# A six-layer cross network on one core: a new order of the first units, a new way of loading x0, and a merged last addition

## The chip, the cores and the metric

The kernel runs on one core of a Trainium2 chip. The metric is the device time of one execution in microseconds (us); the kernel before takes 142.92 us, the median of three runs (142.19 to 143.85). The core has a matrix engine (TensorE, PE in the profile, with its weight loads as PEld), a vector engine (VectorE, DVE), a scalar engine (ScalarE, ACT), GpSimd (POOL) and a sync engine (SP) that here only issues DMAs. Each engine takes its instructions in order. Sixteen DMA engines move the data.

## The reference

The inputs are `x0` (4096 rows of 416 columns, bfloat16), `ws` (6 layers of 416 x 416) and `bs` (6 x 416).

```python
x = x0
for l in range(6):
    x = x0 * (x @ ws[l] + bs[l]) + x
```

## The kernel before

The first five layers work on the transposed x: columns lie on the partitions, rows of x0 along the free dimension. The 416 columns are three planes of 128 (`XM`, planes k = 0, 1, 2) and a remainder of 32 columns. The 4096 rows are two halves, s = 0 and 1, of 2048; a half is four groups g of 512 rows. The remainder columns of a half's four groups stand below each other on the 128 partitions (`XR`). There are three buffers of `XM` and `XR`: number 0 holds x0 itself, 1 and 2 are written by turns, layer by layer.

One **unit** is one layer on one half. For each output plane m it makes 12 matrix products of 512 columns (`mm_full`, line 167: four groups, three input planes) and four products with the 32 remainder rows of the weights, which run side by side on quarters of the array (`mm_row`, line 172). Then come the remainder's own products (`mm_rem`, lines 178 and 183), with `WD` holding the 32 x 32 corner of the weights at the right place. Results collect in PSUM, in four slots of two banks each that all tiles share (`psum`, tag `ps`): a plane takes two slots (two groups in each), the remainder one. The elementwise work of half a plane (`ew_main`, lines 154 to 156) is a ScalarE pass that adds the bias and moves PSUM to a tile `t` of which there are four, a VectorE multiplication by x0, and a VectorE addition of x.

The order of units is layer by layer: (0, first half), (0, second half), (1, first half) and so on, ten units. The first half of x0 is loaded by rows (`X0rows`, four blocks of 512 rows) and transposed on TensorE in the first unit (`x0_transposes_main`, line 125, with copies on VectorE and ScalarE, lines 127 and 129; `x0_transposes_rem`, line 136). Of the second half, planes 0 and 1 come from DRAM through a DMA transpose (line 96), and plane 2 and the remainder come from a slab of 160 columns (`slab1`, line 94) that TensorE transposes late in the first unit (`x0_transposes_k2_s1`, line 144). The rows of the second half follow later, for the last layer only.

The last layer works on rows, because its output is stored by rows. A **quad** is 512 rows; there are four per half. For each quad TensorE makes products with x as the stationary operand (lines 258, 264 and 267, the last adding the bias), ScalarE copies PSUM to `t` (282), VectorE multiplies by `X0rows` (283), adds the three planes from `XLrows` (284) and the remainder from `scrR` (285), and SP stores (286), for half a quad at a time; the last quad goes by quarters (289 to 293). `XLrows` and `scrR` are x after layer 4, brought back to rows by DMA transposes within SBUF: per half three of 128 x 2048 (line 190) and one of 128 x 512 for the remainder (line 242). All are issued by SP, in line with the stores. Outputs go through ten buffers `o`.

The order of instructions on each engine is set by the framework's scheduler, which reorders by its own estimate of readiness; the written order is a preference. Seven matrix products on constant data (`pe_filler`, line 74) run before the first rows land.

## Time and profile before

| | us |
|---|---|
| runs: median (lowest to highest) | 142.92 (142.19 to 143.85) |
| profiled execution, first to last instruction (span) | 141.9 |
| TensorE busy | 130.0 |
| VectorE busy | 109.3 |
| ScalarE busy | 87.0 |
| first evacuation of a product | 17.28 |
| second unit begins | 26.16 |
| third unit begins | 35.99 |
| last layer begins on TensorE | 114.63 |
| last VectorE instruction ends | 138.96 |

The profile names no time of the profiled execution other than its span; the median of the runs lies 1.0 above it, and this difference holds what stands around the span and the variation from run to run. Times in the profile count from the start of the span. The chain of waits gives, for each moment, the piece of work whose end released the next one. An idle engine costs nothing unless it stands in that chain.

### The profile page before, as it was taken

The page shows a single profiled execution, that of the slowest core. Times are in us where ns is not written, and L with a number is a line of the kernel's source. Part 1 is how long each engine was busy: PE and PEld are TensorE (multiplying, and loading weights), DVE is VectorE, ACT ScalarE, POOL GpSimd, SP SyncE. Part 2 cuts the span into 40 slices and gives each one's busy share as a digit, 9 for nine tenths or more (in the row PEclk, how much of TensorE's full clock was granted, in tenths as well). Part 3 has the DMA queues.
Part 4 walks back from the last instruction along what each step waited for, and adds up shares of the span by engine and source line. Part 5 has one row for each costly group of instructions (what it writes and reads, how often), then busy time and mean ns, then how long its engine had stood idle before and what let it go on. Part 6 is the DMA issues. An engine that isn't in the chain of part 4 may idle for free.

```text
span 141.9 us, 2405 instructions
## 1 busy us (share of the span) xinstructions
PE 130.0 (92%) x910; PEld 56.0 (39%) x910; DVE 109.3 (77%) x207; ACT 87.0 (61%) x97; POOL 8.4 (6%) x21
## 2 busy tenths in 40 slices
PE   5759998999999999999999999999999999999910
PEld 2426345434343343343333433433433345445400
DVE  1214178769878888898798799787987989999891
ACT  4011593875695695677657956956776578548530
POOL 8950000000000000000000000000000000000000
PEclk9968999999999999999999999999999999999995
DMA  4999999980000000000000000000089999965542
GB/s 136 294 280 130 232 249 273 330 251 10 0 2 0 0 7 0 0 0 0 0 5 0 0 0 0 5 0 0 0 166 173 146 200 187 229 226 178 175 162 92
DMA packets 31899, 14.69 MB, mean 104 GB/s; under 512 B 20618, under 2 KB 31888, under 8 KB 31888
## 3 DMA queue, kind: packets, MB, share of 16 engines
q1 hardware_dynamic: 31472, 14.38, 43.1%
q0 software_dynamic: 416, 0.16, 0.5%
q8 instruction: 7, 0.11, 0.3%
q14 instruction: 4, 0.03, 0.1%
HBM read 6.68 MB, written 3.41 MB: 71 GB/s over the span
## 4 chain that ended last, share of the span: by engine, by line
PE 71%; DVE 11%; DMA 9%; ACT 3%; issue 2%; SPq 1%; DVEq 0%
DMA X0rows<-in_x_dram 6%; PE pr L183 5%; DMA out_dram<-o 3%; PE pr L178 2%; DVE t L283 2%; DVE XM_87 L156 2%; DVE t L155 2%; DVE o L284 2%; ACT XM_86 L129 1%; PE pt_1184 L167 1%; PE pt_1166 L167 1%; PE pt_1081 L167 1%; PE pt_982 L167 1%; PE pt_784 L167 1%; PE pt_388 L167 1%
## 5 line engine op out<-in xcount | busy, mean ns | idle before, releaser
L167 PEld LDWEIGHTS <-WM 128*128 128x128 bf16 x360 | 33.7, 98 | 45.4 <-issue 8.6
L155 DVE TENSOR_TENSOR t<-t,XM_86 128x1024 bf16<-128x1024 bf16 x60 | 41.2, 686 | 13.5 <-ACT t L154 12.9
L156 DVE TENSOR_TENSOR XM_87<-t,XM_88 128x1024 bf16<-128x1024 bf16 x24 | 16.6, 690 | 2.1
L156 DVE TENSOR_TENSOR XM_88<-t,XM_87 128x1024 bf16<-128x1024 bf16 x24 | 16.6, 691 | 1.4
L258 PEld LDWEIGHTS <-XM_87 128*128 128x128 bf16 x96 | 9.0, 98 | 8.5 <-issue 1.8
L127 DVE COPY XM_86<-tp 128x512 bf16<-128x512 bf16 x8 | 3.3, 422 | 9.3 <-PE tp L125 9.3
L129 ACT COPY XM_86<-tp 128x512 bf16<-128x512 bf16 x4 | 2.3, 585 | 11.6 <-PE tp L125 11.6
L283 DVE TENSOR_TENSOR t<-t,X0rows 128x832 bf16<-128x832 bf16 x14 | 8.2, 586 | 0.9 <-ACT t L282 0.8
L156 DVE TENSOR_TENSOR XM_87<-t,XM_86 128x1024 bf16<-128x1024 bf16 x12 | 8.3, 690 | 0.3
L284 DVE TENSOR_TENSOR o<-t,XLrows 128x768 bf16<-128x768 bf16 x14 | 7.8, 557 | 0.5
L125 PE MATMUL tp<-ident,X0rows 128*128 128x128 bf16 x48 | 5.2, 250 | 2.9 <-DMA X0rows<-in_x_dram 1.7
L160 ACT ACTIVATE t<-pr,bR 128x512 bf16<-128x512 f32 x10 | 6.9, 689 | 0.0
L125 PEld LDWEIGHTS <-X0rows 128*128 128x128 bf16 x48 | 3.9, 114 | 5.5 <-DMA X0rows<-in_x_dram 2.8
L172 PEld LDWEIGHTS <-WR 32*128 32x128 bf16 x120 | 2.4, 91 | 8.4 <-issue 8.1
L74 PE MATMUL wps<-warm 128*128 128x512 bf16 x7 | 3.2, 630 | 1.5 <-DVE dz L67 1.5
L161 DVE TENSOR_TENSOR t<-t,XR_89 128x512 bf16<-128x512 bf16 x10 | 4.2, 418 | 0.0
L183 PEld LDWEIGHTS <-WM 128*32 128x32 bf16 x120 | 3.2, 97 | 2.2
L183 PE MATMUL pr<-XM_88,WM 128*32 128x512 bf16 x48 | 3.3, 379 | 0.0
L183 PE MATMUL pr<-XM_87,WM 128*32 128x512 bf16 x48 | 3.3, 379 | 0.0
L167 PE MATMUL pt_141<-XM_86,WM 128*128 128x512 bf16 x6 | 2.8, 544 | 0.1
L149 ACT COPY XM_86<-tk 128x1024 bf16<-128x1024 bf16 x1 | 1.0, 1012 | 2.3 <-PE tk L144 2.3
L92 POOL DMA_DIRECT2D WD<-in_ws_dram x4 | 2.3, 573 | 0.9 <-DMA WR<-in_ws_dram 0.9
(288 smaller groups left out, 255.4 us busy)
## 6 DMA issues: line engine op xcount, KB each, us to landing
out_dram<-o SPq DMA_DIRECT2D x14, 208.0 KB, 2.2
WM<-in_ws_dram SPq DMA_DIRECT2D x6, 312.0 KB, 6.0
X0rows<-in_x_dram SPq DMA_DIRECT2D x4, 416.0 KB, 7.5
X0rows<-in_x_dram SPq DMA_DIRECT2D x2, 832.0 KB, 8.8
slab_85<-in_x_dram SPq DMA_DIRECT2D x1, 640.0 KB, 10.9
WR<-in_ws_dram SPq DMA_DIRECT2D x4, 130.0 KB, 6.4
out_dram<-o SPq DMA_DIRECT2D x4, 104.0 KB, 1.7
WR<-in_ws_dram POOLq DMA_DIRECT2D x4, 26.0 KB, 5.7
```

The source lines that it names most:

```text
L125: nc.tensor.transpose(tp[:, k, 128 * i:128 * i + 128], X0rows[:, bt, 128 * k:128 * k + 128], ident[:])
L127: nc.vector.tensor_copy(XM[0][:, k, c0:c0 + CW], tp[:, k, :])
L129: nc.scalar.copy(XM[0][:, k, c0:c0 + CW], tp[:, k, :])
L155: nc.vector.tensor_tensor(out=t[:], in0=t[:], in1=XM[0][:, m, c0:c0 + 2 * CW], op=ALU.mult)
L156: nc.vector.tensor_tensor(out=nxt[:, m, c0:c0 + 2 * CW], in0=t[:], in1=cur[:, m, c0:c0 + 2 * CW], op=ALU.add)
L160: nc.scalar.activation(tr[:, 0:CW], pr[:], ACT.Identity, bias=bR[:, l:l + 1], scale=1.0)
L161: nc.vector.tensor_tensor(out=tr[:, 0:CW], in0=tr[:, 0:CW], in1=XR[0][:, CW * s:CW * s + CW], op=ALU.mult)
L167: nc.tensor.matmul(pts[g // 2][:, g % 2, :], lhsT=WM[:, l, k, 128 * m:128 * m + 128], rhs=cur[:, k, c0:c0 + CW], start=(first and k == 0), ...
L183: nc.tensor.matmul(pr[32 * g:32 * g + 32, :], lhsT=WM[:, l, k, NK * P:D], rhs=cur[:, k, c0:c0 + CW], start=False, stop=(k == NK - 1), tile ...
L258: nc.tensor.matmul(py[g // 2][:, g % 2, 0:D], lhsT=cur[:, k, q_cols(q, g)], rhs=WM[:, l, k, :], start=((not rem_first) and k == 0), stop=( ...
L283: nc.vector.tensor_tensor(out=tv, in0=tv, in1=x0v, op=ALU.mult)
L284: nc.vector.tensor_tensor(out=o[:, :, 0:KD], in0=tv[:, :, 0:KD], in1=xlv, op=ALU.add)
```

## The change

Rows are numbered anew. In the first half, partition p of a block of 512 holds four consecutive rows of x0 (3,328 contiguous bytes) where it held four rows 128 apart (four pieces of 832 bytes); the output is written back by the same numbering. The first block is loaded in two DMAs. The second half is loaded as rows too, in four blocks, ahead of the DMA transposes of its planes 0 and 1; the slab is gone, and plane 2 and the remainder are transposed from these rows. Layer 1's weights and the remainder rows of the weights of layers 1 to 5 move ahead of both. `WD` is filled by GpSimd copies out of `WR` in place of four DMAs.

The units go (0, first), (1, first), (0, second), (1, second), and then layer by layer as before. A unit that follows the same half's previous layer directly (`same_half`, two such units) takes the products of planes 0 and 1 first, of output plane 0 and of half of output plane 1, and then those of plane 2. TensorE's transposes of the second half move from the first unit into the second. The filler products are five, and two more behind the first block's transposes. A block's transposes go by rows first, and VectorE copies two planes at once.

For the last layer, the remainder is brought back to rows by four DMA transposes of 32 x 512 per half, into columns 384 to 415 of a wider `XLrows`, so that one addition serves all 416 columns.

`tc.manual_schedule()` turns the reordering off: each engine runs its instructions in the written order.

The core of the diff; the removed loop over layers and halves is printed above, from line 193.

```diff
-    x0_v = x0.rearrange("(bt p) d -> p bt d", p=P)
-    out_v = out.rearrange("(bt p) d -> p bt d", p=P)
+    x0_v = [x0[0:SW, :].rearrange("(c p j) d -> p c j d", p=P, j=4),
+            x0[SW:B, :].rearrange("(c j p) d -> p c j d", p=P, j=4)]
+    out_v = [out[0:SW, :].rearrange("(c p j) d -> p c j d", p=P, j=4),
+             out[SW:B, :].rearrange("(c j p) d -> p c j d", p=P, j=4)]
...
-    XLrows = big.tile([P, NBT, NK * P], BF16)
-    scrR = [big.tile([P, 4, P], BF16, name=f"scrR{s}") for s in range(NS)]
-    slab1 = big.tile([P, 16, 160], BF16)
+    XLrows = big.tile([P, NBT, D], BF16)
...
+    ctx.enter_context(tc.manual_schedule())
...
-    pe_filler(7)
+    pe_filler(5)
...
-    nc.sync.dma_start(X0rows[:, 0:4, :], x0_v[:, 0:4, :])
+    def load_x0(c, j0=0, j1=4):
+        nc.sync.dma_start(X0rows[:, 4 * c + j0:4 * c + j1, :], x0_v[c // 4][:, c % 4, j0:j1, :])
+
+    load_x0(0, 0, 2)
+    load_x0(0, 2, 4)
     load_wm(0)
-    nc.sync.dma_start(X0rows[:, 4:8, :], x0_v[:, 4:8, :])
-    nc.sync.dma_start(X0rows[:, 8:12, :], x0_v[:, 8:12, :])
-    nc.sync.dma_start(X0rows[:, 12:16, :], x0_v[:, 12:16, :])
+    for c in range(1, 4):
+        load_x0(c)
     nc.gpsimd.dma_start(bsb[:], bs[:, :])
     for g in range(NG):
         nc.gpsimd.dma_start(WR[32 * g:32 * g + 32, 0, :], ws[0, NK * P:D, :])
     nc.gpsimd.memset(WD[:], 0.0)
-    with nc.allow_non_contiguous_dma(reason="tiny corner blocks"):
-        for g in range(NG):
-            nc.gpsimd.dma_start(WD[32 * g:32 * g + 32, :, g, :], ws[:, NK * P:D, NK * P:D].rearrange("l r n -> r l n"))
-    with nc.allow_non_contiguous_dma(reason="320B row segments"):
-        nc.sync.dma_start(slab1[:], x0_v[:, 16:32, 2 * P:D])
+    load_wm(1)
+    for g in range(NG):
+        nc.sync.dma_start(WR[32 * g:32 * g + 32, 1:L, :], ws[1:L, NK * P:D, :].rearrange("l r n -> r l n"))
+    for c in range(4, 8):
+        load_x0(c)
     for k in range(2):
         nc.sync.dma_start_transpose(out=XM[0][:, k, SW:2 * SW], in_=x0[SW:2 * SW, 128 * k:128 * k + 128])
-    load_wm(1)
-    for g in range(NG):
-        nc.sync.dma_start(WR[32 * g:32 * g + 32, 1:L, :], ws[1:L, NK * P:D, :].rearrange("l r n -> r l n"))
     for l in range(2, L):
         load_wm(l)
-    nc.sync.dma_start(X0rows[:, 16:24, :], x0_v[:, 16:24, :])
-    nc.sync.dma_start(X0rows[:, 24:32, :], x0_v[:, 24:32, :])
+    for g in range(NG):
+        nc.gpsimd.tensor_copy(WD[32 * g:32 * g + 32, 0, g, :], WR[32 * g:32 * g + 32, 0, NK * P:D])
     for g in range(NG):
         nc.gpsimd.dma_start(bLr[32 * g:32 * g + 1, :], bs[LL:LL + 1, :])
+    for g in range(NG):
+        nc.gpsimd.tensor_copy(WD[32 * g:32 * g + 32, 1:LL, g, :], WR[32 * g:32 * g + 32, 1:LL, NK * P:D])
 
...
-        tp = psum.tile([P, NK, CW], BF16, tag="ps", name="tp")
+        tg = psum.tile([P, 4 * CW], BF16, tag="ps", name="tg")
         c0 = col0(0, g)
-        for k in range(NK):
-            for i in range(4):
-                bt = 4 * g + i
-                nc.tensor.transpose(tp[:, k, 128 * i:128 * i + 128], X0rows[:, bt, 128 * k:128 * k + 128], ident[:])
-            if k < 2:
-                nc.vector.tensor_copy(XM[0][:, k, c0:c0 + CW], tp[:, k, :])
-            else:
-                nc.scalar.copy(XM[0][:, k, c0:c0 + CW], tp[:, k, :])
+        for i in range(4):
+            for k in range(NK):
+                c = CW * k + 128 * i
+                nc.tensor.transpose(tg[:, c:c + 128], X0rows[:, 4 * g + i, 128 * k:128 * k + 128], ident[:])
+        nc.vector.tensor_copy(XM[0][:, 0:2, c0:c0 + CW], tg[:, 0:2 * CW].rearrange("p (k c) -> p k c", k=2))
+        nc.scalar.copy(XM[0][:, 2, c0:c0 + CW], tg[:, 2 * CW:3 * CW])
...
-                src = X0rows[:, 4 * g + i, NK * P:D] if s == 0 else slab1[:, 4 * g + i, P:P + R]
-                nc.tensor.transpose(tpr[32 * g:32 * g + 32, 128 * i:128 * i + 128], src, ident[:],
+                nc.tensor.transpose(tpr[32 * g:32 * g + 32, 128 * i:128 * i + 128],
+                                    X0rows[:, 16 * s + 4 * g + i, NK * P:D], ident[:],
                                     tile_position=(0, 32 * g))
...
-        for h in range(2):
-            tk = psum.tile([P, 2 * CW], BF16, tag="ps", name="tk")
+        tk = psum.tile([P, 2, 2 * CW], BF16, tag="ps", name="tk")
+        for h in range(2):
             for j in range(8):
-                nc.tensor.transpose(tk[:, 128 * j:128 * j + 128], slab1[:, 8 * h + j, 0:P], ident[:])
+                nc.tensor.transpose(tk[:, h, 128 * j:128 * j + 128], X0rows[:, 16 + 8 * h + j, 2 * P:3 * P], ident[:])
             c0 = SW + 2 * CW * h
             if h == 0:
-                nc.vector.tensor_copy(XM[0][:, 2, c0:c0 + 2 * CW], tk[:])
+                nc.vector.tensor_copy(XM[0][:, 2, c0:c0 + 2 * CW], tk[:, h, :])
             else:
-                nc.scalar.copy(XM[0][:, 2, c0:c0 + 2 * CW], tk[:])
+                nc.scalar.copy(XM[0][:, 2, c0:c0 + 2 * CW], tk[:, h, :])
...
+    def mm_full(l, s, m, h, pts, cur, n0, n1, started, last):
+        ks = (2, 0, 1) if (l == 0 and s == 1) else (0, 1, 2)
+        for g in (2 * h, 2 * h + 1):
+            c0 = col0(s, g)
+            for n in range(n0, n1):
+                k = ks[n]
+                nc.tensor.matmul(pts[h][:, g % 2, :], lhsT=WM[:, l, k, 128 * m:128 * m + 128], rhs=cur[:, k, c0:c0 + CW],
+                                 start=(not started and n == n0), stop=(last and n == n1 - 1))
+
+    def mm_row(l, s, m, pts, curR, started, last):
         for g in range(NG):
             nc.tensor.matmul(pts[g // 2][:, g % 2, :], lhsT=WR[32 * g:32 * g + 32, l, 128 * m:128 * m + 128],
                              rhs=curR[32 * g:32 * g + 32, CW * s:CW * s + CW],
-                             start=first, stop=last, tile_position=(32 * g, 0))
+                             start=not started[g // 2], stop=last[g // 2], tile_position=(32 * g, 0))
...
+    def new_pt(name):
+        return psum.tile([P, 2, CW], FP32, tag="ps", name=name)
+
+    units = [(0, 0), (1, 0), (0, 1), (1, 1)] + [(l, s) for l in range(2, LL) for s in range(NS)]
+    before = None
+    for l, s in units:
+        cur, curR = (XM[0], XR[0]) if l == 0 else (XM[1 + (l - 1) % 2], XR[1 + (l - 1) % 2])
         nxt, nxtR = XM[1 + (l % 2)], XR[1 + (l % 2)]
         feeds_last = (l == LL - 1)
+        same_half = before == (l - 1, s)
+
+        if (l, s) == (0, 0):
+            pts0 = [new_pt("pt0"), new_pt("pt1")]
+            x0_transposes_main(0)
+            pe_filler(2)
+            x0_transposes_main(1)
+            def mm_g(g):
+                for k in range(NK):
+                    nc.tensor.matmul(pts0[g // 2][:, g % 2, :], lhsT=WM[:, l, k, 0:128], rhs=cur[:, k, CW * g:CW * g + CW],
+                                     start=(k == 0), stop=False)
+            mm_g(0)
+            bias_setup()
+            x0_transposes_main(2)
+            mm_g(1)
+            x0_transposes_main(3)
+            mm_g(2)
+            x0_transposes_rem(0)
+            mm_g(3)
+        elif same_half:
+            pts0 = [new_pt("pt0"), new_pt("pt1")]
             for h in range(2):
-                ew_main(l, s, 0, h, pts0[h], cur, nxt)
-            if feeds_last:
-                xl_dmat(s, 0, nxt)
+                mm_full(l, s, 0, h, pts0, cur, 0, 2, False, False)
+            pts1 = [new_pt("pt0"), None]
+            mm_full(l, s, 1, 0, pts1, cur, 0, 2, False, False)
+            for h in range(2):
+                mm_full(l, s, 0, h, pts0, cur, 2, 3, True, False)
+            mm_full(l, s, 1, 0, pts1, cur, 2, 3, True, False)
+            pts1[1] = new_pt("pt1")
+        else:
+            pts0 = [new_pt("pt0"), new_pt("pt1")]
+            for h in range(2):
+                mm_full(l, s, 0, h, pts0, cur, 0, 3, False, False)
+        mm_row(l, s, 0, pts0, curR, (True, True), (True, True))
+        if not same_half:
+            pts1 = [new_pt("pt0"), new_pt("pt1")]
+        mm_row(l, s, 1, pts1, curR, (same_half, False), (same_half, False))
...
+        for h in range(2):
+            ew_main(l, s, 0, h, pts0[h], cur, nxt)
+        if feeds_last:
+            xl_dmat(s, 0, nxt)
+        for h in range(2):
+            if not (same_half and h == 0):
+                mm_full(l, s, 1, h, pts1, cur, 0, 3, True, True)
+        pts2 = [new_pt("pt0"), new_pt("pt1")]
+        for h in range(2):
+            mm_full(l, s, 2, h, pts2, cur, 0, 3, False, False)
+        for h in range(2):
+            ew_main(l, s, 1, h, pts1[h], cur, nxt)
+        if feeds_last:
+            xl_dmat(s, 1, nxt)
+        if (l, s) == (1, 0):
+            x0_transposes_k2_s1()
+            x0_transposes_rem(1)
+        mm_row(l, s, 2, pts2, curR, (True, True), (True, True))
+        pr = psum.tile([P, CW], FP32, tag="ps", name="pr")
+        mm_rem(l, s, pr, cur, curR)
+        for h in range(2):
+            ew_main(l, s, 2, h, pts2[h], cur, nxt)
+        ew_rem(l, s, pr, curR, nxtR)
+        if feeds_last:
+            xl_dmat(s, 2, nxt)
             for g in range(NG):
-                mm_full(l, s, 1, g, pts1, cur, False, True)
-            pts2 = new_pts()
-            for g in range(NG):
-                mm_full(l, s, 2, g, pts2, cur, True, False)
-            for h in range(2):
-                ew_main(l, s, 1, h, pts1[h], cur, nxt)
-            if feeds_last:
-                xl_dmat(s, 1, nxt)
-            if first_unit:
-                x0_transposes_k2_s1()
-                x0_transposes_rem(1)
-            mm_row(l, s, 2, pts2, curR, False, True)
-            pr = psum.tile([P, CW], FP32, tag="ps", name="pr")
-            mm_rem(l, s, pr, cur, curR)
-            for h in range(2):
-                ew_main(l, s, 2, h, pts2[h], cur, nxt)
-            ew_rem(l, s, pr, curR, nxtR)
-            if feeds_last:
-                xl_dmat(s, 2, nxt)
-                nc.sync.dma_start_transpose(out=scrR[s][:], in_=nxtR[:, CW * s:CW * s + CW])
-        cur, curR = nxt, nxtR
+                nc.sync.dma_start_transpose(out=XLrows[:, 16 * s + 4 * g:16 * s + 4 * g + 4, NK * P:D],
+                                            in_=nxtR[32 * g:32 * g + 32, CW * s:CW * s + CW])
+        before = (l, s)
+    cur, curR = nxt, nxtR
...
-            bts = [16 * s + 4 * (2 * h + gl) + i for gl in range(2)]
+            c = 4 * s + 2 * h
+            bts = [4 * c + i, 4 * c + 4 + i]
             t = tpool.tile([P, 2 * CW], BF16, name="t")
             tv = t[:, 0:2 * D].rearrange("p (a d) -> p a d", a=2)
             o = opool.tile([P, 2, D], BF16, name="o")
-            x0v = X0rows[:, bts[0]:bts[1] + 1:4, :]
-            xlv = XLrows[:, bts[0]:bts[1] + 1:4, :]
-            xrv = scrR[s][:, i, 64 * h:64 * h + 64].rearrange("p (a r) -> p a r", a=2)
             if not last_quad:
                 nc.scalar.copy(tv, py[h][:, :, 0:D])
-                nc.vector.tensor_tensor(out=tv, in0=tv, in1=x0v, op=ALU.mult)
-                nc.vector.tensor_tensor(out=o[:, :, 0:KD], in0=tv[:, :, 0:KD], in1=xlv, op=ALU.add)
-                nc.vector.tensor_tensor(out=o[:, :, KD:D], in0=tv[:, :, KD:D], in1=xrv, op=ALU.add)
-                nc.sync.dma_start(out_v[:, bts[0]:bts[1] + 1:4, :], o[:])
+                nc.vector.tensor_tensor(out=tv, in0=tv, in1=X0rows[:, bts[0]:bts[1] + 1:4, :], op=ALU.mult)
+                nc.vector.tensor_tensor(out=o[:], in0=tv, in1=XLrows[:, bts[0]:bts[1] + 1:4, :], op=ALU.add)
+                nc.sync.dma_start(out_v[s][:, 2 * h:2 * h + 2, i, :], o[:])
             else:
                 for gl in range(2):
                     nc.scalar.copy(tv[:, gl, :], py[h][:, gl, 0:D])
                     nc.vector.tensor_tensor(out=tv[:, gl, :], in0=tv[:, gl, :], in1=X0rows[:, bts[gl], :], op=ALU.mult)
-                    nc.vector.tensor_tensor(out=o[:, gl, 0:KD], in0=tv[:, gl, 0:KD], in1=XLrows[:, bts[gl], :], op=ALU.add)
-                    nc.vector.tensor_tensor(out=o[:, gl, KD:D], in0=tv[:, gl, KD:D], in1=xrv[:, gl, :], op=ALU.add)
-                    nc.sync.dma_start(out_v[:, bts[gl], :], o[:, gl, :])
+                    nc.vector.tensor_tensor(out=o[:, gl, :], in0=tv[:, gl, :], in1=XLrows[:, bts[gl], :], op=ALU.add)
+                    nc.sync.dma_start(out_v[s][:, 2 * h + gl, i, :], o[:, gl, :])
```

31 lines of the change are left out of this document (2 added, 29 removed).

## The prediction

> **What bounds the kernel now.** I read the page's busy line first, then the chain that ended last in order of time, to cut the span into stages, then each stage's busy time.
>
> ```profile
> span 141.9 us, 2405 instructions
> PE 130.0 (92%) x910; PEld 56.0 (39%) x910; DVE 109.3 (77%) x207; ACT 87.0 (61%) x97; POOL 8.4 (6%) x21
> ```
>
> The chain (start, length, what); its DMA row ends the wait for the first half's last rows:
>
> ```profile
> 2.86 9.17 DMA X0rows<-in_x_dram
> ...
> 16.83 0.39 PE pt_141 L172 x2
> ...
> 17.28 1.10 ACT t L154
> ...
> 26.16 1.40 PE pt_370 L167 x6
> ...
> 35.99 1.40 PE pt_469 L167 x6
> ...
> 104.80 1.40 PE pt_1166 L167 x6
> ...
> 113.65 0.33 PE pr L178 x4
> ...
> 114.63 1.16 PE pt_1269 L258 x6
> ...
> 138.87 0.09 DVE o L292
> ```
>
> A unit is one layer on one half. Nine units run from 26.16 to 114.63 at 9.83 each. Before them stands the first unit with the loads and transposes, behind them the last layer, which ends on VectorE and the stores. The stages (start:end, length, busy time per engine, clock, DMA share, GB/s):
>
> ```profile
> 5.05:8.45 3.40, 1.04 (x16) 0.70 (x14) 1.09 (x4) 0.58 (x1) 2.51 (x5) 1.00 1.03 310
> 8.45:11.90 3.45, 3.03 (x16) 1.76 (x16) 1.10 (x3) 0.00 (x0) 1.50 (x4) 0.51 1.22 230
> ...
> 35.99:104.80 68.81, 68.81 (x451) 27.36 (x450) 59.59 (x98) 47.76 (x50) 0.00 (x0) 1.00 0.03 6
> 119.70:124.90 5.20, 5.20 (x43) 2.62 (x41) 4.82 (x13) 3.26 (x5) 0.00 (x0) 1.00 0.98 240
> 123.00:125.00 2.00, 2.00 (x13) 1.11 (x12) 1.72 (x6) 1.86 (x3) 0.00 (x0) 1.00 1.02 326
> ```
>
> From the third row on TensorE is never idle, and the change takes no product out, so those stages can't shrink. What can move is the 35.99 us ahead of the third unit, and the tail. In the first row TensorE idles for want of data, in the second it works at half clock.
>
> **The loads.** Two issues on SP, and times from issue to landing (last figure):
>
> ```profile
> 1.25 0.49 SPq L79 DMA_DIRECT2D WM<-in_ws_dram  x1
> 1.79 0.48 SPq L83 DMA_DIRECT2D X0rows<-in_x_dram  x1
> ```
>
> ```profile
> WM<-in_ws_dram SPq DMA_DIRECT2D x1, 312.0 KB, 3.8
> X0rows<-in_x_dram SPq DMA_DIRECT2D x1, 416.0 KB, 7.0
> WD<-in_ws_dram POOLq DMA_DIRECT2D x4, 12.0 KB, 5.5
> ```
>
> Layer 0's weights land at 5.05, the second x0 block at 8.8 (3.75 later), the fourth at 12.03 (1.6 per block). The bytes queued ahead of block 2 stay as they are. What goes: four WD loads of 64-byte pieces on POOL's queue, and behind the blocks the 320-byte slab and both DMA transposes; a partition's piece grows from 832 to 3,328 bytes. POOL's four WR loads stay. So block 2 lands between 5.05 + 1.6 = 6.65 and today's 8.8. I take 7.0, 8.6 and 10.2 for blocks 2 to 4, nearer the early end since most small pieces go. SP's one extra issue (0.48) lies beside bytes in flight.
>
> **TensorE up to the first evacuation.** Prices of its pieces and of the evacuation copies:
>
> ```profile
> 12.08 0.51 PE L125 MATMUL tp<-ident,X0rows 128*128 128x128 bf16 x6
> ...
> 22.57 1.06 PE L144 MATMUL tk<-ident,slab_85 128*128 128x128 bf16 x16
> ...
> 23.73 0.68 DVE L147 COPY XM_86<-tk 128x1024 bf16<-128x1024 bf16 x1
> ...
> 24.46 0.41 PE L136 MATMUL tpr<-ident,slab_85 128*32 128x128 bf16 x16 [0.51 <-DVE XM_86 L147]
> ```
>
> Twelve transposes of a block cost 1.04, three products 0.7 (1.40 for six), the 16 corners 0.41; I set 0.3 for the seven bias transposes, an estimate below the 16 corners. In the written order: block 2 from 7.0 to 8.05, products of group 0 to 8.75, bias to 9.05, block 3 to 10.1, group 1 to 10.8, block 4 (landed 10.2) to 11.85, group 2 to 12.55, corners to 12.95, group 3 to 13.65, row products 0.45 (16.83 to 17.28). The copies (0.68, one wide one for two) lie under the next group's products, 0.7; without that cover each costs its 0.68. First evacuation: 14.1, against 17.28.
>
> **From there to the third unit.** Evacuation and elementwise work of a regular unit, the one from 104.80:
>
> ```profile
> 107.86 1.11 ACT L154 ACTIVATE t<-pt_1166,bM 128x1024 bf16<-128x1024 f32 x1 [1.30 <-PE pt_1167 L172]
> 109.00 0.69 DVE L155 TENSOR_TENSOR t<-t,XM_86 128x1024 bf16<-128x1024 bf16 x1 [0.64 <-ACT t L154]
> 109.80 0.69 DVE L156 TENSOR_TENSOR XM_87<-t,XM_88 128x1024 bf16<-128x1024 bf16 x1
> 110.41 0.68 DVE L155 TENSOR_TENSOR t<-t,XM_86 128x1024 bf16<-128x1024 bf16 x1
> ...
> 113.69 1.11 ACT L154 ACTIVATE t<-pt_1211,bM 128x1024 bf16<-128x1024 f32 x1 [1.70 <-PE pt_1212 L172]
> ```
>
> From first evacuation to unit end is 114.63 - 107.86 = 6.8: unit (layer 1, first half) ends at 20.9. The next unit now reads what that one wrote. Its last column plane is late: evacuation ends at +0.2 after the unit, then two multiply-add pairs of 1.41 (0.80 and 0.61): +3.1. Meanwhile TensorE has twelve products on planes 0 and 1 and two on the plane's first part, 3.2. I charge 0.1; without that cover it would be 3.1. The same again at unit (2, second half).
>
> This unit also takes the second half's transposes, 1.06 + 0.41. Its first evacuation comes after six more products, at 3.06 + 1.4 = 4.5; VectorE starts 1.14 later, does four pairs (5.65) and then the third-plane copy, 0.68: 11.95. Only then is the PSUM slot free for the remainder products, which TensorE reaches at 9.83 - 0.98 + 0.1 + 1.47 = 10.4. Wait 1.5 (zero if another slot is free, so 0 to 1.5). Length 9.83 + 0.1 + 1.47 + 1.5 = 12.9: the third unit starts at 33.8, against 35.99. Less 0.1 for the second dependent unit, gain 2.1.
>
> Edits that cost nothing, with their cover: the two DMA transposes of the second half now stand behind more bytes. Behind block 4 come layer 1's weights (0.32 MB), WR (0.53), the second half (1.7) and the transposes (1.05), 3.6 MB from 10.2 on: landed at 21.8 by the 310 GB/s of the first window, at 25.9 by the 230 of the second, due at 33.8. If that cover were gone, the wait would stand in full ahead of unit (1, second half). The corner copies into WD make POOL wait for WR; the remainder products need them at 19.9 and 32.8, and the bias-row loads queued behind the first of them on POOL are due only in the last layer. The fillers, five and two for seven, run where TensorE has no data. The order of every engine is now the written one; where I see it bind is the copy above.
>
> **Tail.** SP's transposes feeding the last layer, and one landing:
>
> ```profile
> 110.16 1.56 SPq L242 DMA_TRANSPOSE scrR_83<-XR_90  x1
> ...
> 111.92 4.75 SPq L190 DMA_TRANSPOSE XLrows<-XM_87  x2
> ...
> 117.88 2.17 SPq L190 DMA_TRANSPOSE XLrows<-XM_87  x1
> ...
> 120.15 1.39 SPq L242 DMA_TRANSPOSE scrR_84<-XR_90  x1
> ```
>
> ```profile
> scrR_84<-XR_90 SPq DMA_TRANSPOSE x1, 2.6
> ```
>
> ```profile
> 118.88 0.56 DVE L284 TENSOR_TENSOR o<-t,XLrows 128x768 bf16<-128x768 bf16 x1
> 119.36 0.19 DVE L285 TENSOR_TENSOR o<-t,scrR_83 128x64 bf16<-128x64 bf16 x1
> 119.46 0.58 DVE L283 TENSOR_TENSOR t<-t,X0rows 128x832 bf16<-128x832 bf16 x1
> ...
> 129.15 0.56 DVE L284 TENSOR_TENSOR o<-t,XLrows 128x768 bf16<-128x768 bf16 x1
> ```
>
> ```profile
> L283 DVE TENSOR_TENSOR t<-t,X0rows 128x832 bf16<-128x832 bf16 x14 | 8.2, 586 | 0.9 <-ACT t L282 0.8
> ```
>
> One add for two saves 0.10 and adds 64 columns, some 0.05: 0.05 per half-quad. TensorE hides all but those behind its last product; 0.2 gained.
>
> Against it, each half has four remainder transposes of 32 partitions for one of 128, and the wide add now waits for all four, with all of VectorE's queue behind it. With SP held h by each, the second half's last one lands at 110.16 + 4h + 4.75 + 2.17 + 4h + 0.7 of gaps - h + 2.6 = 120.4 + 7h; the add at 129.15 (today's clock, all shifts alike) needs it. h is unseen: at least 1.39/4 if it goes by size, 1.56 if not; the rows for 1.39 (128x512) and 2.17 (128x2048) make a line that gives 1.2. I take it: landed at 128.8, cost nothing. At 1.56 it lands at 131.3; some 0.7 of that is taken up by VectorE's waits (0.8 in the last row), cost 1.5. The Trainium skill speaks against this edit: DMA: Bandwidth & Descriptors, under Rules for kernel authors, wants small transfers merged, since below 64 KB one pays mostly overhead; each piece here has 32 KB. By that the 1.56 end would hold, and the sum would be 142.1. Stores queue behind on SP: 3.4 MB at 326 GB/s take 10.5 us from about 127.6, done when the last results come; ten output buffers cover the delay.
>
> **Sum.** 2.1 + 0.2 = 2.3 us off the profiled 141.9: 139.6. The median of the runs, 142.92, is 1.0 above that span: 140.6.
>
> **Rivals.** *Half clock and late rows* (0.27). In the first window TensorE was busy 1.04 of 3.4 us, and half clock followed for 3.45. After the change it is busy there about 1.4, little more. With block 2 at 7.5 and the clock halved from 8.45 to 11.9, products double to 1.3 and transposes of a block to 1.3: first evacuation at 15.6, 1.5 later than forecast, 142.1; with today's landings (8.8, 10.4, 12.03) 16.8 and 143.3. Against it stands only that those landings come earlier. The Trainium skill, TensorE: Matmul & The Clock Gate, Part 1: an idle window of about 3.4 us halves the clock, a busy one restores it; the two windows agree. By it either clock is possible (140.6 or 142.1): whether 1.4 busy counts as idle no run here shows.
>
> *Better still* (0.13). Block 2 at 6.65 (0.35 earlier) and no wait for the PSUM slot (1.5): 1.85 less, 138.8. For it: nothing but the four WR loads is left beside the x0 blocks; against: which slot the remainder products get follows the order of release, and the copy's comes first.
>
> *SP becomes the bound, slower* (0.12). If a small transpose holds SP as long as the large one, h = 2.17, the last lands at 135.6, VectorE and then TensorE stall 5.7 net, 146.3. It decides against the change from h = 1.9 (cost 3.8, 144.4). For: four instructions for one; against: 1.39 for a bigger piece.
>
> *The reorder does nothing by itself*: today's transposed planes land before 26.16 without anyone waiting, so layers 1 and 2 first is worth 0, or minus the 0.2 of dependent units; it is inside every case.
>
> **Numbers.** Forecast case 0.48 (139.6 to 141.4). Range 138.7 to 143.4: it takes in better and half clock, and leaves out SP and half of the extremes, together under 0.2. A difference of 1% (141.5 to 144.35 is the same) is about what can be told. Faster: 0.46 of the forecast case, 0.13, 0.02 of the half clock: 0.61. Same: 0.27. Slower: 0.12.
>
> **What would show it.** Block 2's first transpose near 7.0; first evacuation near 14.1; PEclk 1.00 from 8.45 to 11.9; the third unit at 33.8 with one wait of 1.5 before the remainder products; waits near 0.1 at the dependent units; SP held about 1.2 per small transpose and no VectorE wait on DMA at quad 4. I am wrong if rows land as late as now, or if SP's last remainder transpose comes after 129 on this clock.

## The result and the profile after

The changed kernel takes 147.22 us, the median of four runs (146.18 to 148.14); the kernel before took 143.38 (142.19 to 144.44) beside it. The ratio is 1.031, with a 95% interval of 1.023 to 1.039: slower, where 140.6 was forecast. A ratio and its interval leave out executions that lie more than 1.5% above the quickest of the same kernel, so where the executions spread, a ratio is not that of the two medians. The profiled execution took 146.5 us, 2.0 more than its span.

The first lines of the page after, which answer to those of before:

```profile
span 144.5 us, 2395 instructions
PE 129.6 (90%) x910; PEld 55.6 (38%) x910; DVE 109.2 (76%) x185; ACT 87.0 (60%) x97; POOL 8.1 (6%) x25
```

No engine is busy longer than before (VectorE 109.2 us against 109.3); the 2.6 us that the span is longer are waiting. The chain that ended last (start, length, what), with the starts of the second and third unit and of the last layer, and VectorE's last instruction:

```profile
20.58 3.60 PE pt L172 x16
...
31.52 0.61 DVE XM L149
32.13 0.04 issue
32.17 0.62 PE tk L146 x8
...
35.78 3.43 PE pt L172 x12
...
115.19 2.22 PE pt L288 x12
...
138.99 0.38 DVE o L318
```

The start was good: the second unit begins at 20.58, before it was 26.16. Of these 5.6 us the earlier first evacuation makes 3.5 (13.80 against 17.28); the other 2.1 are the second half's transposes and their wait, which have only moved into the second unit. By the third unit only 0.21 us of that is left (35.78 against 35.99), the last layer starts 0.56 late, and behind VectorE's last instruction (139.37, before 138.96) the span goes on for 5.1 us, where it was 2.9. So there are two places, the second unit and the end.

The second unit, by the timeline (start, length, engine, line, what, and in brackets the idle time before it and who ended it):

```profile
7.63 0.84 PE L129 MATMUL tg<-ident,X0rows 128*128 128x128 bf16 x12 [1.73 <-DMA X0rows<-in_x_dram]
...
13.80 4.13 ACT L156 ACTIVATE t<-pt,bM 128x1024 bf16<-128x1024 f32 x4 [0.48 <-PE pt L177]
...
28.98 0.61 PE L146 MATMUL tk<-ident,X0rows 128*128 128x128 bf16 x8
...
31.43 0.68 DVE L149 COPY XM<-tk 128x1024 bf16<-128x1024 bf16 x1
32.17 0.61 PE L146 MATMUL tk<-ident,X0rows 128*128 128x128 bf16 x8 [2.58 <-DVE XM L149]
...
32.81 1.01 ACT L151 COPY XM<-tk 128x1024 bf16<-128x1024 bf16 x1 [3.72 <-PE tk L146]
...
33.88 0.62 PE L183 MATMUL pr<-XR,WD 128*32 128x512 bf16 x4 [0.44 <-ACT XM L151]
34.26 1.52 PE L188 MATMUL pr<-XM,WM 128*32 128x512 bf16 x12
```

The change made one PSUM tile `tk` of the two that held eight plane-2 transposes each. Now the second eight wait until VectorE has copied the first eight out, and that copy stands in VectorE's queue behind the unit's multiply-add pairs: 2.58 us of an idle TensorE. Then ScalarE, idle for 3.72 until they come, copies them, and that holds the remainder products for 0.44. The twelve products of line 188 take 1.52, where the same twelve (line 183 there) took 0.82 before; the granted clock of this stretch, in the stages below, is 0.74: the clock has fallen.

```profile
25.34 0.82 PE L183 MATMUL pr<-XM_86,WM 128*32 128x512 bf16 x12
```

The end, by SP's issues (start, time in which SP is held, what):

```profile
110.50 5.72 SPq L270 DMA_TRANSPOSE XLrows<-XR  x4
116.31 7.90 SPq L195 DMA_TRANSPOSE XLrows<-XM  x3
124.30 5.72 SPq L270 DMA_TRANSPOSE XLrows<-XR  x4
130.12 8.37 SPq L313 DMA_DIRECT2D out_dram<-o  x14
138.57 2.52 SPq L319 DMA_DIRECT2D out_dram<-o  x4
```

Four small transposes hold SP for 5.72 us, 1.43 each on average, where one of 128 x 512 held it for 1.39 to 1.56. The first store goes out at 130.12; before it was 121.63:

```profile
121.63 14.92 SPq L286 DMA_DIRECT2D out_dram<-o  x14
```

What that does to the DMA engines stands in the stages (start:end, length, busy time per engine, clock, DMA share, GB/s), first after:

```profile
32.20:35.60 3.40, 2.96 (x44) 1.33 (x43) 0.24 (x1) 2.79 (x4) 0.00 (x0) 0.74 0.02 5
35.60:39.00 3.40, 3.40 (x16) 1.27 (x12) 3.20 (x6) 1.31 (x2) 0.00 (x0) 0.76 0.00 0
...
121.60:130.00 8.40, 8.40 (x71) 4.11 (x70) 7.39 (x14) 5.02 (x7) 0.00 (x0) 1.00 0.60 121
132.00:140.00 8.00, 3.88 (x33) 1.69 (x31) 7.00 (x16) 3.35 (x6) 0.00 (x0) 0.98 1.04 327
```

and the same eight microseconds, 132 to 140, before:

```profile
132.00:140.00 8.00, 3.32 (x30) 1.41 (x28) 6.51 (x23) 3.35 (x6) 0.00 (x0) 0.88 0.53 172
```

Before, the stores kept pace with VectorE at 172 GB/s; now all 3.41 MB leave behind 130 at 327 GB/s, with the DMA engines full, and the last results queue behind earlier ones. From the start of the last layer to the end of the span: 27.3 us before, 29.3 after.

### The profile page after: what moved, and what is told of

Read it like the earlier page. It is cut to its first block, busy times and chain, and to the rows that moved or that the text cites. A ratio compares the mean times of both kernels' runs of the same rounds, so it can differ in the third digit from the quotient of the medians.

```text
span 144.5 us, 2395 instructions
## 1 busy us (share of the span) xinstructions
PE 129.6 (90%) x910; PEld 55.6 (38%) x910; DVE 109.2 (76%) x185; ACT 87.0 (60%) x97; POOL 8.1 (6%) x25
## 3 DMA queue, kind: packets, MB, share of 16 engines
HBM read 5.97 MB, written 3.41 MB: 65 GB/s over the span
## 4 chain that ended last, share of the span: by engine, by line
PE 80%; DVE 7%; DMA 4%; ACT 3%; issue 1%; SPq 1%; ACTq 0%
PE pt L172 51%; PE pt L288 11%; PE pt L177 6%; PE pr L188 5%; DMA X0rows<-in_x_dram 4%; PE pr L183 2%; DVE XM L158 2%; DVE t L157 2%; PE tg L129 2%; PE pt L294 1%; DVE t L317 1%; PE pt L297 1%; PE pt L216 1%; DVE o L318 1%; ACT t L156 1%
## 5 line engine op out<-in xcount | busy, mean ns | idle before, releaser
L156 ACT ACTIVATE t<-pt,bM 128x1024 bf16<-128x1024 f32 x60 | 62.5, 1113 | 30.3 <-PE pt L177 30.3
L172 PE MATMUL pt<-XM,WM 128*128 128x512 bf16 x348 | 79.2, 382 | 0.0
L157 DVE TENSOR_TENSOR t<-t,XM 128x1024 bf16<-128x1024 bf16 x60 | 41.2, 687 | 14.6 <-ACT t L156 13.8
L158 DVE TENSOR_TENSOR XM<-t,XM 128x1024 bf16<-128x1024 bf16 x60 | 41.5, 692 | 4.6
L288 PE MATMUL pt<-WM,XM 128*128 128x416 bf16 x96 | 17.7, 340 | 0.0
L310 ACT CAST t<-pt 128x832 bf16<-128x832 f32 x14 | 11.3, 856 | 6.7 <-PE pt L297 6.2
L288 PEld LDWEIGHTS <-XM 128*128 128x128 bf16 x96 | 9.0, 98 | 8.5 <-issue 1.8
L177 PE MATMUL pt<-XR,WR 32*128 32x512 bf16 x120 | 10.1, 381 | 0.1
L312 DVE TENSOR_TENSOR o<-t,XLrows 128x832 bf16<-128x832 bf16 x14 | 8.3, 592 | 1.0 <-DMA XLrows<-XR 0.5
L188 PE MATMUL pr<-XM,WM 128*32 128x512 bf16 x120 | 8.9, 405 | 0.0
```

Of the source, the lines that this page charges most:

```text
L156: nc.scalar.activation(t[:], pt[:].rearrange("p a b -> p (a b)"), ACT.Identity, bias=bM[:, m, l:l + 1], scale=1.0)
L157: nc.vector.tensor_tensor(out=t[:], in0=t[:], in1=XM[0][:, m, c0:c0 + 2 * CW], op=ALU.mult)
L158: nc.vector.tensor_tensor(out=nxt[:, m, c0:c0 + 2 * CW], in0=t[:], in1=cur[:, m, c0:c0 + 2 * CW], op=ALU.add)
L172: nc.tensor.matmul(pts[h][:, g % 2, :], lhsT=WM[:, l, k, 128 * m:128 * m + 128], rhs=cur[:, k, c0:c0 + CW], start=(not started and n == n0 ...
L177: nc.tensor.matmul(pts[g // 2][:, g % 2, :], lhsT=WR[32 * g:32 * g + 32, l, 128 * m:128 * m + 128], rhs=curR[32 * g:32 * g + 32, CW * s:CW ...
L188: nc.tensor.matmul(pr[32 * g:32 * g + 32, :], lhsT=WM[:, l, k, NK * P:D], rhs=cur[:, k, c0:c0 + CW], start=False, stop=(k == NK - 1), tile ...
```

## The experiments

Each time is the median of four to ten executions; each ratio is against the kernel before, timed in turn with it.

**Two tiles again.**

```diff
-        tk = psum.tile([P, 2, 2 * CW], BF16, tag="ps", name="tk")
         for h in range(2):
+            tk = psum.tile([P, 2 * CW], BF16, tag="ps", name="tk")
```

> The changed kernel with one edit: the 16 transposes of the second half's plane 2 go to two PSUM tiles, eight each, as in the kernel before, not to one tile of two banks. Theory A (the merged tile makes TensorE's second eight wait for VectorE's copy of the first eight, 2.6 us, and the idling halves the clock after it): the wait of 2.6 between the two eights goes, one wait of about 2 for a PSUM slot stands in its place ahead of the corner transposes, the clock stays full, the third unit starts near 34.0 instead of 35.78 and the one after it takes 9.8 instead of 10.6: 2.2 us less, 145.0, ratio to the kernel before 1.016. Rival (the slot wait alone costs as much, because VectorE reaches that copy only at 31.4 anyway): third unit at 35.5 or later, 147 and 1.03.

Measured: 145.99 us, ratio 1.025 (1.015 to 1.034). Its timeline:

```profile
8.02 0.84 PE L129 MATMUL tg<-ident,X0rows 128*128 128x128 bf16 x12 [2.13 <-DMA X0rows<-in_x_dram]
9.95 1.46 PE L129 MATMUL tg<-ident,X0rows 128*128 128x128 bf16 x12
...
15.68 2.12 ACT L156 ACTIVATE t<-pt,bM 128x1024 bf16<-128x1024 f32 x2 [0.48 <-PE pt L177]
...
30.85 1.06 PE L146 MATMUL tk<-ident,X0rows 128*128 128x128 bf16 x16
34.05 0.41 PE L137 MATMUL tpr<-ident,X0rows 128*32 128x128 bf16 x16 [2.14 <-DVE XM L149]
```

The wait of 2.58 is gone, but one of 2.14 stands one step later: the corner transposes need a slot, and VectorE's late copy still holds it. The clock stays full behind it (twelve products in 0.82). From first evacuation to third unit it is 20.1 us, in the changed kernel 22.0. The start was worse in this execution: block 3 was transposed at half clock (1.46 for 0.84), and the first evacuation came 1.9 later. That ate the gain in this profile: its third unit begins at 35.76. The time lies half way between the two expectations, and the ratio's interval overlaps that of the changed kernel (1.023 to 1.039), so by the times alone no gain is shown. The shorter stretch is what the trace shows.

**One remainder transpose per half.** As before the change: 128 x 512 into `scrR`, and the addition split in two.

```diff
-            for g in range(NG):
-                nc.sync.dma_start_transpose(out=XLrows[:, 16 * s + 4 * g:16 * s + 4 * g + 4, NK * P:D],
-                                            in_=nxtR[32 * g:32 * g + 32, CW * s:CW * s + CW])
+            nc.sync.dma_start_transpose(out=scrR[s][:], in_=nxtR[:, CW * s:CW * s + CW])
```

> The changed kernel with the remainder brought back to rows by one DMA transpose of 128 x 512 per half, and two additions, as in the kernel before. Theory B (eight small transposes hold SP, which issues the first store at 130 instead of 122, and the stores then drain at the DMA engines' rate behind the last result): first store at about 123, last store lands about 2 us after the last addition, 2.2 us less, 145.0, ratio 1.016. Rival (the stores are slower because of the new row numbering, or the end is set elsewhere): DMA busy without a gap up to the end as now, 147, 1.03; the split additions alone would cost 0.2 more.

Measured: 145.62 us, ratio 1.018 (1.012 to 1.024). SP and the stage at the end:

```profile
121.56 1.48 SPq L270 DMA_TRANSPOSE scrR<-XR  x1
123.14 15.00 SPq L314 DMA_DIRECT2D out_dram<-o  x14
```

```profile
132.00:140.00 8.00, 4.91 (x39) 2.25 (x37) 7.50 (x24) 4.00 (x7) 0.00 (x0) 1.00 0.52 173
```

The stores start at 123.14 and keep pace again, at 173 GB/s. From the start of the last layer to the end it is 27.3 us again, in all six profiles of kernels with one remainder transpose per half and the new row numbering; in the four with small transposes and all stores on SP it is 29.3 to 29.8. So the loss at the end is due to the four small transposes, and not to the new numbering of the rows. The additions are split in the same edit, but VectorE's wait for the last remainder had been only 0.49 us.

**Both of these.**

> Both edits: two PSUM tiles, and one remainder transpose per half. Theories A and B together, each with its own place: gains add, 4.4 less, 142.8, ratio 0.997. If one of the two only uncovers the other: 144.5 to 145, 1.01.

Measured: 144.02 us (ten runs, 141.34 to 145.25), ratio 0.995 (0.989 to 1.001); the median of all ten lies 0.8% above that of the kernel before (142.93). With both undone, the rest of the change is worth nothing that can be told. The spread of 3.9 us is wide; the profiled execution had the half clock at the start.

**Stores of the first half issued by GpSimd**, in the changed kernel, so that they need not stand behind the transposes on SP.

```diff
-                nc.sync.dma_start(out_v[s][:, 2 * h:2 * h + 2, i, :], o[:])
+                (nc.gpsimd if s == 0 else nc.sync).dma_start(out_v[s][:, 2 * h:2 * h + 2, i, :], o[:])
```

> The changed kernel, all eight small transposes kept, but the stores of the first half's rows are issued by GpSimd, so that they do not stand behind the transposes on SP. Theory B (what costs is the place of the stores in SP's queue, not the transposes or the wide addition): stores begin near 120, and the end comes about 1.7 to 2.2 us earlier, 145.2, 1.017. Rival (the late remainder transposes and the wide addition that waits for them cost the time): 147, 1.03.

Measured: 147.55 us, ratio 1.034 (1.026 to 1.043): no gain. SP, GpSimd and VectorE:

```profile
116.44 9.53 SPq L195 DMA_TRANSPOSE XLrows<-XM  x3
126.07 6.49 SPq L270 DMA_TRANSPOSE XLrows<-XR  x4
...
120.61 0.76 POOL L313 DMA_DIRECT2D out_dram<-o  x1 [106.02 <-DVE o L312]
...
133.50 0.59 DVE L312 TENSOR_TENSOR o<-t,XLrows 128x832 bf16<-128x832 bf16 x1 [3.82 <-DMA XLrows<-XR]
```

The stores begin at 120.61, but beside them the three large transposes take 9.53 instead of 7.90 and the small ones 6.49 instead of 5.72, and now VectorE waits 3.82 for the last remainder. One bound takes the place of the other; the time in the small transposes is what has to go.

**The order of the instructions.** The changed kernel without the written order:

```diff
-    ctx.enter_context(tc.manual_schedule())
```

> This is the changed kernel without the line that fixes the written order of the instructions, so the framework orders them again, as it did before the change; loads, transposes and tiles are those of the changed kernel. Theory (the loss sits in the remainder transposes on SP and in the shared PSUM tile, not in who orders the instructions): the four 1.43 us transposes of each half and the shared tile are still there, so 146 to 148 us, first store again near 130 us. Rival (the written order itself costs the time): 144 us or less, with the unit behind the second half's transposes starting before 34 us for a first evacuation at 13.8.

Measured: 147.37 us, ratio 1.029 (1.025 to 1.033). Its second eight:

```profile
34.38 0.61 PE L145 MATMUL tk<-ident,X0rows 128*128 128x128 bf16 x8 [1.68 <-DVE XM L148]
```

The framework pulled the corner transposes and some products ahead of them, but they still wait for VectorE's copy out of the shared tile. In this profile the stretch from first evacuation to third unit takes 20.2 us, where the written order took 22.0, but the last layer takes 29.8, and the first evacuation came at 16.05. By the medians, who orders is no cause here. The reverse, the kernel before with the written order:

> The kernel before, with the one line of the change that keeps the instructions in the written order, and nothing else. Theory (who orders the instructions is worth little here, as the changed kernel without that line showed): 142.5 to 144.5, within 1 per cent of before. Rival (the written order of before costs or gains by its own): outside of that.

Measured: 148.58 us, ratio 1.037 (1.031 to 1.044), 5.2 us slower, far outside what the theory allowed. TensorE and VectorE at the second block, and the stages:

```profile
8.45 0.61 PE L127 MATMUL tp<-ident,X0rows 128*128 128x128 bf16 x4 [1.55 <-DMA X0rows<-in_x_dram]
...
9.09 0.42 DVE L129 COPY XM<-tp 128x512 bf16<-128x512 bf16 x1 [1.90 <-PE tp L127]
...
9.57 0.58 PE L127 MATMUL tp<-ident,X0rows 128*128 128x128 bf16 x4 [0.51 <-DVE XM L129]
```

```profile
7.90:11.30 3.40, 1.82 (x13) 1.40 (x14) 0.85 (x2) 0.01 (x1) 1.95 (x4) 0.50 1.23 254
11.30:14.70 3.40, 2.37 (x13) 1.32 (x12) 0.85 (x2) 0.57 (x1) 0.00 (x0) 0.50 1.33 197
```

In its written order a plane's four transposes wait 0.5 us for the copy of the plane before, which lies in the same PSUM tile; TensorE is busy 1.82 of 3.40 us and works at half clock. The scheduler put products into these gaps. All of the loss lies ahead of the first evacuation, which comes at 22.33 where it was 17.28; from there on the stretches are as long as before. The changed kernel gained nothing by reordering; that this is because of its wide blocks of twelve transposes, with products written between them, is argued and not shown.

**Both plane-2 copies on ScalarE**, added to the kernel with both mends.

```diff
-            if h == 0:
-                nc.vector.tensor_copy(XM[0][:, 2, c0:c0 + 2 * CW], tk[:])
-            else:
-                nc.scalar.copy(XM[0][:, 2, c0:c0 + 2 * CW], tk[:])
+            nc.scalar.copy(XM[0][:, 2, c0:c0 + 2 * CW], tk[:])
```

> This is the kernel with both mends (two PSUM tiles for the plane-2 transposes, one remainder transpose per half), with both plane-2 copies on ScalarE instead of one on VectorE. Theory (the corner transposes wait 2.1 us only because VectorE comes late to the first copy, behind its arithmetic of the unit): that wait falls to about 0.5 us, the third unit starts about 1.5 us earlier against the same first evacuation (some 18.6 us after it instead of 20.1), and the time is about 142.5 us where the kernel with both mends had 144.0. Rival (ScalarE's own evacuations are pushed back by two copies of about 1.0 us each, so another wait of the same length comes): third unit still 20 us after the first evacuation, 144 us.

Measured: 141.14 us (140.57 to 143.42), ratio 0.984 (0.979 to 0.988): quicker than both kernels. The same stretch, and SP's first store:

```profile
14.29 3.12 ACT L154 ACTIVATE t<-pt,bM 128x1024 bf16<-128x1024 f32 x3 [0.48 <-PE pt L175]
...
31.18 0.41 PE L138 MATMUL tpr<-ident,X0rows 128*32 128x128 bf16 x16 [0.65 <-ACT XM L149]
...
33.07 2.76 PE L170 MATMUL pt<-XM,WM 128*128 128x512 bf16 x11
...
118.70 15.03 SPq L311 DMA_DIRECT2D out_dram<-o  x14
```

The wait is 0.65 (0.5 expected), the third unit starts 18.8 us behind the first evacuation (18.6 expected). The time came out 1.4 below what was expected, and 2.9 below the median of the kernel with both mends, where 1.5 was expected; but by the two ratios (0.995 and 0.984) the step is 1.6. In the profiles 1.2 us of it lie between first evacuation and third unit (20.09 against 18.85), and 1.6 are an earlier first evacuation (14.29 against 15.86), which differs from one execution to the next.

**Fillers behind the first block**, seven for two, in that kernel and in the changed kernel alone.

> The kernel before this one in the list (both mends, both plane-2 copies on ScalarE) with seven instead of two filler products of TensorE behind the first block's transposes, 6.3 to 8 us into the span, which keep TensorE busy while it waits for the second block. They compute nothing that is used. Theory (the spread of these kernels comes from a clock that falls to half in that gap in some executions and not in others): the transposes of blocks 3 and 4 run at full clock in all executions, the first evacuation comes at 13.8 to 14.2, the times lie closer together (within 1.5 us), and the median is about 141 us, 1 to 2 below the same kernel with two fillers. Rival (the fillers only delay the second block, whose transposes now begin after 8.5 us, or the clock falls all the same): no gain, or up to 0.5 us slower.

> The changed kernel with seven instead of two filler products behind the first block's transposes, nothing else. Theory (half clock early in some executions makes the spread of 146.2 to 148.1): all executions look like the quickest, about 146.2 to 146.5 us with a spread under 1 us, first evacuation at 13.8 to 14.2; it stays slower than before, since the store drain and the wait in the second unit are untouched. Rival (the early clock has no part in the time, since the later waits absorb it): 147.2 us and the same spread.

Measured: 141.02 (140.69 to 141.96), ratio 0.987 (0.981 to 0.992), and 146.74, ratio 1.023 (1.018 to 1.027). The medians fall by 0.1 and 0.5, no more than the measurement can tell. The gain of 1 to 2 us that the theory gave did not come. The spread narrows from 2.9 to 1.3 us in the first pair and from 2.0 to 0.7 in the second, leaving out one execution of 462 us (below). That is four executions each: ten of a kernel further down, with seven fillers too, spread over 2.3 us, so it is not shown that the fillers narrow it.

**One mend without the other.** The two tiles with ScalarE's copies, but with the four small transposes:

> The changed kernel with two PSUM tiles for the plane-2 transposes, both copied by ScalarE; the eight small remainder transposes of the last layer stay. Theory (two losses that add: the wait in the second unit and the late stores): the third unit starts about 18.8 us behind the first evacuation, 2 to 3 us earlier than in the changed kernel (35.8), everything behind it moves by as much, the stores too, and the time is 143.8 to 144.8, some 3 us above the kernel with both mends and both copies on ScalarE. Rival (the late stores set the end by themselves, and an earlier last layer only makes them wait): 146 us or more.

Measured: 144.29 us, ratio 1.006 (1.002 to 1.011), as the theory said: the late stores add to the rest, they don't swallow it. The other way round, one remainder transpose and seven fillers, with the shared tile:

> The changed kernel with one remainder transpose per half and seven filler products behind the first block, the shared PSUM tile left as it is. The two mends gained 2.9 us (tiles and copies alone, 147.2 to 144.3) and 1.6 us (remainder alone, 147.2 to 145.6), but 6.1 us together. Theory (the missing 1.6 is the half clock before the first evacuation, which came at 15.2 in the profile of the kernel with the remainder mend alone and at 13.8 in that of the changed kernel): with the fillers the first evacuation comes at 13.8 to 14.2 and the time is 144.0 to 144.7. Rival (the two mends help each other, whatever the clock): about 145.6 with the first evacuation at 13.8 to 14.2, or the fillers don't hold the clock.

Measured: 143.9 us, ratio 1.004 (0.999 to 1.009). By medians the two mends gave 2.9 and 1.6 alone and 6.1 together; with seven fillers the remainder mend gave 2.8, and tiles and copies behind it 2.9. The profiles tell why the medians don't add cleanly. Cut into four stretches, they show each mend in a stretch of its own, with the same length to 0.4 us whatever the other mend and whenever the first evacuation came (us; the four make the span, to the rounding):

| kernel | to first evacuation | to third unit | to last layer | to the end |
|---|---|---|---|---|
| before | 17.28 | 18.71 | 78.6 | 27.3 |
| changed | 13.80 | 21.98 | 79.4 | 29.3 |
| two tiles | 15.68 | 20.08 | 78.7 | 29.5 |
| one remainder transpose | 15.21 | 21.98 | 79.0 | 27.3 |
| both | 15.86 | 20.09 | 78.7 | 27.3 |
| two tiles, copies on ScalarE | 17.33 | 18.85 | 78.7 | 29.6 |
| one remainder transpose, seven fillers | 14.83 | 21.98 | 79.1 | 27.3 |
| both, copies on ScalarE | 14.29 | 18.85 | 78.7 | 27.3 |

So tiles and copies are worth 3.1 us up to the third unit and 0.4 to 0.7 behind it, the remainder transpose 2.0 to 2.3 at the end, and these add. The first evacuation lies up to 3.7 us apart (13.66 to 17.33) in profiles of kernels that load alike, about as much as either mend is worth, and the medians carry that. It moves with block 2's landing and with the clock: in the row with seven fillers the clock was full and the evacuation yet came at 14.83, since block 2 landed at 8.57. Against the kernel before, the last row gains in the first stretch alone.

**The old order of units**, in the quickest kernel, with the second half's transposes back in the first unit.

```diff
-    units = [(0, 0), (1, 0), (0, 1), (1, 1)] + [(l, s) for l in range(2, LL) for s in range(NS)]
+    units = [(l, s) for l in range(LL) for s in range(NS)]
...
-        if (l, s) == (1, 0):
+        if (l, s) == (0, 0):
```

> The quickest kernel so far (141.1: two PSUM tiles, both plane-2 copies on ScalarE, one remainder transpose per half) with the order of units of before: layer 1 of both halves, then layer 2 of both, with the plane-2 and corner transposes of the second half back in the first unit. The loads and the DMA transposes stay. Theory (the new order is what hides the second half's planes 0 and 1): these two are issued at 12.6 and 19.8 us and land at about 22 to 24.5, while the unit of the second half would now begin at 20 to 22; TensorE waits 1 to 3 us there, its clock falls, and the kernel takes 142.5 to 144.5. Rival (the order is worth nothing once the two planes come by DMA, since they land just in time and no dependent unit follows its own layer): 141 us, or up to 0.5 less.

Measured: 142.04 us, ratio 0.993 (0.988 to 0.997), between the two expectations:

```profile
24.25 2.32 PE L170 MATMUL pt<-XM,WM 128*128 128x512 bf16 x9 [1.07 <-DMA XM<-in_x_dram]
```

TensorE waits 1.07 us for the planes that come by DMA transpose, at the low end of what the theory gave. The new order hides this; it is worth about 0.9 us behind the new loads, which bring these planes later than the kernel before did, and the clock didn't fall.

## Why the prediction was wrong

The forecast span was 139.6, the measured 144.5. The 4.9 us between them are 2.0 up to the third unit (33.8 forecast, 35.78 measured), 0.7 inside it, and 2.2 in the tail (27.1 forecast, 29.3 measured).

- *Loads and first evacuation: right in the profiled execution, and in part by luck.* Block 2's first transpose 7.63 (7.0 forecast), first evacuation 13.80 (14.1), second unit 20.58 (20.9). Of nine profiles of kernels with these loads and two fillers, four had it at 13.7 to 14.3, and five at 15.2 to 17.3, as the rival of half clock said, to which the prediction gave 0.27. Block 2 was ready between 7.49 and 8.77 in these traces, and the clock fell in some executions and not in others.
- *The second unit: failed, at the step "Only then is the PSUM slot free for the remainder products".* The copy was put at the right place in VectorE's queue (end at 11.95 behind the unit's start forecast, 11.53 measured), but its waiter was wrong. It isn't the remainder products behind the transposes that wait; the second eight transposes do, since they write the same tile. So 2.58 and 0.44 us came for 1.5, with ScalarE's second copy in series, and the unit took 15.2 for 12.9. Some 0.9 us of that is the clock behind the wait (0.62 and 1.28 for the remainder products in the chain, 0.33 and 0.65 elsewhere). The trace of before had shown such a wait, where its three planes of a block share a tile:

```profile
5.57 0.38 PE L125 MATMUL tp<-ident,X0rows 128*128 128x128 bf16 x4 [0.52 <-DVE XM_86 L127]
```

  There the copy follows at once and costs 0.52. In the second unit it stands behind eight instructions of VectorE.
- *The next unit: not in the sum.* Its first twelve products still run at reduced clock, 3.43 for 2.70; this unit takes 10.56 for 9.83.
- *Dependent units: right.* The fourth unit (the second half's second layer) takes 9.87: 0.04 of cost, 0.1 charged.
- *h: mis-sized.* 1.2 was taken from a line through two sizes; 1.43 was measured, near the end of 1.56 that the row for one large transpose gave. VectorE waited only 0.49 for the last remainder, so the term that the prediction hung on h was small, as forecast. That wait ended at 131.29, so the prediction's own sign of being wrong, a last remainder transpose behind 129, came true, but it is not what cost the time. Nor does the wide addition wait for all four pieces, as the prediction had it: the quad's first addition started at 129.71 without a wait, as it needs two of the four, and only the second waited. The Trainium skill (DMA: Bandwidth & Descriptors, Rules for kernel authors) wants transfers of under 64 KB merged. The runs agree: four pieces of 32 KB held SP for 5.72 us, one of 128 KB for 1.48.
- *The stores: failed, at "done when the last results come".* They started at 130.12 for about 127.6, and from there the DMA engines are full to the end. The prediction's own 10.5 us from 130.12 give 140.6, 1.3 behind the last VectorE instruction, before the last stores have landed; the sum held no term for it. One remainder transpose per half removes it: 2.0 to 2.3 us by the stretches of the profiles, by medians 1.6 with two fillers and 2.8 with seven.
- *Median against span: mis-sized.* The 1.0 us added to the span is 2.0 in the changed kernel's profile alone, and the median lies 0.7 above that. In the runs of the kernel before, the time lies 1.7 to 1.9 above the span. By that, an estimate, its profiled execution took 143.7, near the upper end of the three runs (142.19 to 143.85) whose median it was compared with; the forecast took the 1.0 between the two for what stands around the span. This is the other 1.7 of the 6.6 us between 140.6 and 147.22.
- *Rivals.* "SP becomes the bound" had the right place and the wrong mechanism: the stores behind the transposes, not the addition in front of them. "The reorder does nothing by itself" is off by 0.9 us in the mended kernel, whose planes come later than those of the kernel before, which the rival spoke of; in that kernel the new order alone was not run.

That the mended kernel takes 141.1, near the 140.6 forecast, doesn't save the working: it has neither the wait nor the small transposes that the forecast reckoned with.

What stays open is what sets the first evacuation: when block 2 lands, and when the clock falls at the start.

## What to carry to other kernels

Where two buffers are merged into one tile, ask who must wait for the whole tile: each copy out of it becomes a wait for the next writer, and its price is the place of that copy in its engine's queue, so give it to the engine that is idle there. A DMA queue that carries transposes and stores in line needs a term for the stores themselves: first store, bytes, rate, and the landing of the last one. At the sizes seen here, small transposes are priced by their number and not by their size.

## What was not expected of the hardware

- SP's time for a DMA transpose grows far less than its size: 1.43 to 1.57 us on average for 32 x 512 where no store runs beside it, 1.39 to 1.81 for 128 x 512 in these profiles, about 2.6 for 128 x 2048 (7.9 for three).
- Idle time and clock: behind waits of 2.58 and 2.59 us TensorE ran on at reduced clock (twelve remainder products in 1.52, in four profiles of four), behind waits of 1.68 and 2.14 it did not (0.82, in three of three). At the start, the same busy time went with either clock: two windows of the kernel with two tiles, and the same of the one with both copies on ScalarE:

```profile
4.50:7.90 3.40, 1.39 (x8) 0.50 (x5) 0.69 (x1) 0.59 (x1) 0.41 (x2) 1.00 0.93 316
7.90:11.30 3.40, 3.28 (x35) 2.49 (x36) 0.94 (x3) 0.59 (x1) 1.84 (x7) 0.68 1.12 278
```

```profile
4.50:7.90 3.40, 1.41 (x8) 0.50 (x5) 0.69 (x1) 0.59 (x1) 0.59 (x2) 1.00 0.97 335
7.90:11.30 3.40, 3.13 (x39) 2.25 (x41) 1.54 (x4) 0.58 (x1) 1.29 (x5) 1.00 1.10 294
```

  The Trainium skill (TensorE: Matmul & The Clock Gate, Part 1: The HAM clock gate) says that the window which decides runs freely, about 3.4 us long, and isn't bound to the kernel's start. The rows fit that; no run here shows the window itself.
- In one execution of the changed kernel with seven fillers, 462 us long, TensorE was busy for 447.0 us where it is otherwise 129.6, with a granted clock that reads 1.00 (chain of waits, start, length, what):

```profile
8.11 5.72 PE wps L76 x7
...
39.15 14.29 PE pt L172 x17
```

  A product of 512 columns took 0.84 us there (17 in 14.29), about four times the 0.22 of the changed kernel's chain (24 in 5.29). No run explains it.
